# Both projections by w_phi in plain float32, one head per half of the array's rows

## The chip, the cores and the metric

The kernel runs on one core of a Trainium2 chip. The metric is device time in microseconds (us) of one execution; where several runs are given, the median counts. The engines are TensorE (PE, with its weight loads PEld), VectorE (DVE), ScalarE (ACT), GpSimd (POOL) and SyncE (SP), which issues the DMAs.

## The reference

Linear attention with a feature map, followed by a gated feed-forward layer, all in float32:

```python
def phi(x):                                  # x: batch 8, heads 8, sequence 576, head_dim 64
    proj = einsum('bhsd,df->bhsf', x, w_phi) # 128 features
    proj = proj - max(abs(proj), axis=-1)
    return concatenate([exp(proj), exp(-proj)], axis=-1)
q_p, k_p = phi(q), phi(k)
kv = einsum('bhsf,bhsd->bhfd', k_p, v)
z = sum(k_p, axis=2)
x = einsum('bhsf,bhfd->bhsd', q_p, kv) / (einsum('bhsf,bhf->bhs', q_p, z) + 1e-6)
# x reshaped to 4608 tokens x 512
out = (sigmoid(x @ w_gate) * (x @ w_val)) @ w_out   # 1536 hidden features
```

## The kernel before

The 64 heads are worked on in 32 pairs (`b, p`). A pair's Q and K lie with their features in the partitions: head 0 in partitions 0 to 63, head 1 in 64 to 127, the sequence along the free axis (576 for Q; for K four blocks of 128 and a fifth that holds both heads' last 64 positions side by side). `w_phi` is laid out as `wk`, 128 x 384, three blocks of 128 columns: [w; 0], [0; w] and [w; w] (upper half; lower half). The first two keep the heads apart in a product over all 128 partitions, since the zeros drop the other head.

Precision comes in two forms. A plain float32 product shows as two records on PE. A split product takes operands rounded to `F32R` and the remainders, `split(h, l, x)`: ACT copies x into h, rounding it, and DVE subtracts to get l; the product is then a sum of several `F32R` products of one record each.

`att_k(b, p)` (K side). For the first eight pairs (`WHOLE`), each of K's four blocks is one plain product with `wk[:, :256]` (L316), which gives both heads' 128 features for 128 positions. For the other 24 pairs K is split into `kh`, `kl` and each block is three `F32R` products with the split `wq`. Two blocks fill one PSUM bank, so group g = 0 holds blocks 0 and 1 of both heads, g = 1 blocks 2 and 3, and g = 2 the fifth block (L321, plain in all pairs). For each group DVE takes the maximum `mx` (L325) and, after the first four pairs, subtracts it (`dk`, L344); ACT takes the exponentials `ek` (L338 or L350). Ten plain products with V accumulate `kvp` (L358), which is copied, transposed (`tp`, L367) and copied again.

`att_q(b, p)` (Q side). Four pieces: two halves `hf` of the sequence (288 each) times two heads. For the first eight pairs a piece is one plain product with the [w; 0] or [0; w] block (L397). For the others, `s` ("stack", named `sq`) is built for each head: its rounded values in its own 64 partitions (ACT, L387), and the remainders in the other 64 (DVE, L388); two `F32R` products over all 128 partitions, with the two parts of `wq`'s [w; w] block, make the piece (L403). ACT copies each piece to `d` (L407); DVE finds the maxima over features and subtracts them (L413 to L428).

`att_num` multiplies the exponentials of Q by the KV state (`nm`, L456), `att_norm` and `att_scale` divide by the denominator, by way of DRAM for a broadcast, and write x to DRAM (`xs`).

The pool of PSUM banks for both projections, `ps_p`, has three buffers (tag "pp"); a pair takes seven from it, three for K and four for Q.

The feed-forward has 12 blocks of 128 hidden features. The first five (`JA`) run beside the attention as units of `mm_in` (L136, tile `gv`) and `mm_out` (L143, tile `acc`), started when a batch's x is complete; the other seven run after it, over 512 tokens at a time (tiles `g`, `v`, `acc`). The order of instructions on each engine is made by the framework's scheduler from program order and priorities: attention steps are issued under `high_priority` and the feed-forward units, handed out by `fill()`, take the room between. `issue_after(marks...)` holds some scheduling (the weights' unpacking, `att_scale`) behind DVE's subtraction in `att_q`.

Of the kernel before, what the change touches and what calls it, by code (L numbers as in the profile page):

```python
# [8 lines left out]
F32 = mybir.dt.float32  # L9
F32R = mybir.dt.float32r  # L10
# [3 lines left out]
ALU = mybir.AluOpType  # L14
AX = mybir.AxisListType
PSUM = bass.MemoryType.PSUM
DRAM = bass.MemoryType.DRAM

B, H, S, D = 8, 8, 576, 64
F = 128  # L20
P = 128
NP = H // 2
# [8 lines left out]
HS = S // 2  # L31
KVW = D + 1

JA = 5  # feed-forward blocks that run beside the attention
JR = 8  # blocks JA to JR - 1 take the attention's bytes, the others phase 1's
WHOLE = 8  # first pairs: plain float32 products, no splits
DIRECT = 4  # first pairs: K's exponentials straight from PSUM
PRIORITY = 400
RATE, LAG = 0.7, 2  # feed-forward units per slot; slots from x to its first unit


@with_exitstack
def attention_moe(
# [9 lines left out]
    nc = tc.nc  # L53
    vec, act, pool = nc.vector, nc.scalar, nc.gpsimd
# [4 lines left out]
    def split(h, l, x):  # L59
        a = act.copy(h, x)  # L60
        return a, vec.tensor_tensor(l, x, h.bitcast(F32), op=ALU.subtract)  # L61
# [2 lines left out]
        for m in marks:  # L64
            stack.enter_context(tc.issue_after(m.ins))

# [1 line left out]
    weights = {}  # L68

    ebias = const.tile([P, 1], F32, name="ebias")  # L70
    vec.memset(ebias, -896.0 * 2.0**23)

    def from_f64(h, l, raw, mid, sp, nb, name):
        # h: the value cut to 12 bits; l: the other bits as an integer times their unit
        words = raw.rearrange("p (n two) -> p n two", two=2)
        lo, hi = words[:, :, 0], words[:, :, 1]
        top = sp.tile([P, DM], U32, tag="wtop", name="wtop" + name, bufs=nb)
        vec.tensor_scalar(top, hi, 0x7FFFFE00, None, op0=ALU.bitwise_and)
        relu = act.activation(top, top, AF.Relu, bias=ebias, scale=8.0)
        vec.scalar_tensor_tensor(  # L80
            top, hi, 0x80000000, top, op0=ALU.bitwise_and, op1=ALU.bitwise_or
        )
        vec.tensor_copy(h, top.bitcast(F32))
        if mid is None:
            rest, unit = hi, lo
            vec.tensor_scalar(
                hi, hi, 16, 0x01FF0000, op0=ALU.logical_shift_left, op1=ALU.bitwise_and
            )
            vec.scalar_tensor_tensor(
                hi, lo, 16, hi, op0=ALU.logical_shift_right, op1=ALU.bitwise_or  # L90
            )
        else:
            words = mid.rearrange("p (n two) -> p n two", two=2)
            rest, unit = words[:, :, 0], words[:, :, 1]
            vec.tensor_scalar(rest, rest, 0x01FFFFFF, None, op0=ALU.bitwise_and)
        vec.tensor_scalar(unit, top, 0xFF800000, None, op0=ALU.bitwise_and)
        return relu, vec.scalar_tensor_tensor(
            l, rest, 2.0**-36, unit.bitcast(F32), op0=ALU.mult, op1=ALU.mult
        )

    def load_weights(j, m, wp, sp, nb, twice):
        if m == 0:
            wh = wp.tile([P, 3 * DM], F32R, tag=f"wh{j}", name=f"wh{j}")
            wl = wp.tile([P, 3 * DM], F32R, tag=f"wl{j}", name=f"wl{j}")
            weights[j] = (wh, wl)
        wh, wl = weights[j]
        ms = slice(m * DM, m * DM + DM)
        raw = sp.tile([P, 2 * DM], U32, tag="wraw", name=f"wraw{j}_{m}", bufs=nb + 1)
        load, mid = nc.sync.dma_start(raw, w_moe[j, :, m, :].bitcast(U32)), None
        if twice:  # L110
            # the same rows two bytes on: a word then holds the bits below h's
            mid = sp.tile([P, 2 * DM], U32, tag="wmid", name=f"wmid{j}_{m}", bufs=nb)
            nc.sync.dma_start(
                mid[:, : 2 * DM - 1].bitcast(U16),
                w_moe[j, :, m, :].bitcast(U16)[:, 1 : 4 * DM - 1],
            )
        return load, *from_f64(wh[:, ms], wl[:, ms], raw, mid, sp, nb, f"{j}_{m}")
# [135 lines left out]
            xs = nxt  # L253
        out_step(*late)

# [1 line left out]
    with ExitStack() as actx:  # L257
        wp1 = actx.enter_context(tc.tile_pool(name="wp1", bufs=1))
        moe = actx.enter_context(tc.tile_pool(name="moe1", bufs=2))
        at1 = actx.enter_context(tc.tile_pool(name="at1", bufs=1, side="right"))  # L260
        at = actx.enter_context(tc.tile_pool(name="at", bufs=2, side="right"))
        ps_gv = actx.enter_context(tc.tile_pool(name="ps_gv", bufs=2, space=PSUM))
        ps_p = actx.enter_context(tc.tile_pool(name="ps_p", bufs=3, space=PSUM))
# [5 lines left out]
        make_identity(nc, ident)  # L269
        wk = at1.tile([P, 3 * F], F32, name="wk")  # L270
        nc.sync.dma_start(wk, w_phi)
        wq = at1.tile([P, 2, 3 * F], F32R, name="wq")
        split(wq[:, 0, :], wq[:, 1, :], wk)
        dens = [
            dram.tile([2, S], F32, tag=f"den{i}", name=f"den{i}") for i in range(B * NP)
        ]
# [16 lines left out]
        def att_k(b, p):  # L293
            n = f"{b}_{p}"
            kx, vx = loaded.pop(("kv", b, p))
            kvp = ps_kv.tile([KVW, 2, 2 * F], F32, tag="kvp", name="kvp" + n)
            es = []
            whole = b * NP + p < WHOLE
            if not whole:
                kh = at.tile([P, 4 * P], F32R, tag="kh", name="kh" + n, bufs=2)  # L300
                kl = at.tile([P, 4 * P], F32R, tag="kl", name="kl" + n, bufs=2)
                split(kh, kl, kx[:, : 4 * P])
            for g in range(3):
                pp = ps_p.tile([P, 4, F], F32, tag="pp", name=f"pk{n}_{g}")
                if g < 2:
                    ns = 4
                    for i in range(2):
                        o = pp[:, 2 * i : 2 * i + 2, :].rearrange("p a f -> p (a f)")
                        ts = slice((2 * g + i) * P, (2 * g + i + 1) * P)
                        terms = [(kx, wk[:, : 2 * F])] if whole else [  # L310
                            (kh, wq[:, 0, : 2 * F]),
                            (kh, wq[:, 1, : 2 * F]),
                            (kl, wq[:, 0, : 2 * F]),
                        ]
                        for t, (x, w) in enumerate(terms):
                            nc.tensor.matmul(  # L316
                                o, x[:, ts], w, start=t == 0, stop=t == len(terms) - 1
                            )
                else:
                    ns = 1  # L320
                    nc.tensor.matmul(  # L321
                        pp[:, 0, :], kx[:, 4 * P :], wk[:, 2 * F :], start=True, stop=True
                    )
# [7 lines left out]
                    bufs=2 if ns > 1 else 2,  # L331
# [10 lines left out]
                else:  # L342
# [4 lines left out]
                        op=ALU.subtract,  # L347
# [7 lines left out]
            for hd in range(2):  # L355
                for t in range(5):
                    slot = 2 * t + hd
                    nc.tensor.matmul(  # L358
                        kvp[:, hd, :], vx[:, slot, :],
                        es[t // 2][:, slot % 4 if t < 4 else 0, :],  # L360
                        start=t == 0, stop=t == 4,
                    )
            kvt = at.tile([KVW, 4, F], F32, tag="kvt", name="kvt" + n, bufs=1)
# [14 lines left out]
        def att_q(b, p):  # L378
            n = f"{b}_{p}"
            x = loaded.pop(("q", b, p))  # L380
            early = b * NP + p < WHOLE
            if not early:
                s = at.tile([P, 2, S], F32R, tag="stack", name="sq" + n)
                for hd in range(2):
                    own = slice(hd * D, hd * D + D)
                    oth = slice(D - hd * D, P - hd * D)
                    act.copy(s[own, hd, :], x[own])  # L387
                    vec.tensor_tensor(  # L388
                        s[oth, hd, :], x[own], s[own, hd, :].bitcast(F32), op=ALU.subtract
                    )  # L390
            d = at.tile([P, 2, S], F32, tag="d", name="d" + n)
            for hf in range(2):
                for hd in range(2):
                    cs = slice(hf * HS, hf * HS + HS)
                    pp = ps_p.tile([P, HS], F32, tag="pp", name=f"pq{n}_{hf}{hd}")
                    if early:
                        nc.tensor.matmul(  # L397
                            pp, wk[:, hd * F : hd * F + F], x[:, cs],
                            start=True, stop=True,
                        )  # L400
                    else:
                        for i in range(2):
                            nc.tensor.matmul(  # L403
                                pp, wq[:, i, 2 * F :], s[:, hd, cs],
                                start=i == 0, stop=i == 1,
                            )
                    act.copy(d[:, hd, cs], pp)  # L407
            nj = 2 * S // 32
            pm = at.tile([P, nj], F32, tag="pm", name="pm" + n)
            pn = at.tile([P, nj], F32, tag="pn", name="pn" + n)  # L410
# [4 lines left out]
                op=ALU.max, apply_absolute_value=True, apply_transpose=True,  # L415
# [4 lines left out]
            for a in range(4):  # L420
                o = a ^ 1
# [216 lines left out]
```

## Time and profile before

| | |
|---|---|
| median of 3 runs | 1304.68 us (1303.23 to 1305.15) |
| profiled execution, its span | 1307.2 us |
| mean granted TensorE clock | 0.992 |
| PE / PEld busy | 1269.8 / 1070.8 us |
| DVE / ACT busy | 877.5 / 650.7 us |
| DMA moved | 125.12 MB |
| first eight pairs' projections (L397, the last start) | to 124.6 us |
| last projection record (L321, start) | 648.2 us |

The profile is of one execution. Busy time is the union of an engine's records; on PE records overlap, so a record's mean duration is longer than the spacing of a stream of such records. A row of instruction groups reads: line, engine, operation, tiles out<-in, shapes, count | busy us, mean ns of one | idle time of the engine just before them and what ended it. In the shapes of a product, 128*65 stands for a stationary operand of 128 rows and 65 columns. "f32" stands for `F32R` operands too.

### The profile page before, as it was taken

Reading aid. Unit: us, or ns where it says so; the run is one execution under the profiler, and the core shown is the slowest. Engines: PE = TensorE matmul, PEld = TensorE weight load, DVE = VectorE, ACT = ScalarE, POOL = GpSimd, SP = SyncE. Lnnn points to the kernel's source line nnn. Section 1 sums busy time; section 2 is a strip of 40 time slices with the busy share of each in tenths; the row PEclk is TensorE's granted clock in tenths of the full one; section 3 lists DMA queues with packets and bytes.
Section 4 is the critical chain, followed back from the end, with each engine's and each line's share of the span. In section 5 each row is a group of like instructions: output and inputs, shape, how many; then the busy total and the mean of one; then the engine's idle time right before and its main releaser. Section 6 shows DMA issues by size and latency. Waiting matters only on the chain.

```text
span 1307.2 us, 19107 instructions
## 1 busy us (share of the span) xinstructions
PE 1269.8 (97%) x7112; PEld 1070.8 (82%) x7112; DVE 877.5 (67%) x1778; ACT 650.7 (50%) x1416; POOL 0.6 (0%) x6
## 2 busy tenths in 40 slices
PE   7878999999999999999999999999999999999998
PEld 4545788999898989898998988888888888888886
DVE  5777989899899888989866958834343443434333
ACT  5754777777777787777754523322222222222221
POOL 0000000000000000000000000000000000000000
PEclk9988999999999999999999999999999999999999
DMA  5576543233233323332225424313021211202010
GB/s 190 165 216 195 167 131 100 85 107 105 86 115 86 107 84 118 94 108 76 61 69 180 130 78 132 97 65 97 1 97 33 65 50 48 97 1 97 1 65 33
DMA packets 75166, 125.12 MB, mean 96 GB/s; under 512 B 18496, under 2 KB 38080, under 8 KB 75072
## 3 DMA queue, kind: packets, MB, share of 16 engines
q1 hardware_dynamic: 75072, 123.89, 30.7%
q8 instruction: 56, 0.92, 0.3%
q14 instruction: 38, 0.31, 0.1%
HBM read 95.25 MB, written 28.46 MB: 95 GB/s over the span
## 4 chain that ended last, share of the span: by engine, by line
PE 88%; DVE 4%; DMA 4%; ACT 2%; issue 1%; SPq 0%; DVEq 0%; ACTq 0%
PE acc L143 22%; PE gv L136 17%; PE g L136 13%; PE v L136 13%; PE kvp L358 9%; PE nm L456 7%; PE pk L316 3%; PE pq L403 2%; PE pq L397 1%; DMA xs<-xp 1%; DMA q<-q 1%; DMA rb<-den 1%; DMA dn<-ex 1%; ACT ek L338 1%; DMA wraw<-w_moe 1%
## 5 line engine op out<-in xcount | busy, mean ns | idle before, releaser
L136 PE MATMUL gv<-xh,wh 128*128 128x256 f32 x720 | 208.3, 290 | 3.6 <-DVE t L156 3.4
L136 PE MATMUL gv<-xh,wl 128*128 128x256 f32 x720 | 206.5, 287 | 0.0
L136 PE MATMUL gv<-xl,wh 128*128 128x256 f32 x720 | 206.2, 286 | 0.0
L60 ACT CAST hh<-u 128x256 fp32r<-128x256 f32 (+1 forms) x153 | 75.4, 494 | 245.3 <-DVE u L157 245.1
L143 PE MATMUL acc<-wh,hh 128*128 128x512 f32 x432 | 171.3, 397 | 0.7 <-ACT y L187 0.7
L143 PE MATMUL acc<-wl,hh 128*128 128x512 f32 x432 | 169.9, 393 | 0.0
L143 PE MATMUL acc<-wh,hl 128*128 128x512 f32 x432 | 166.1, 394 | 0.1
L358 PE MATMUL kvp<-ek,v 128*65 128x256 f32 x640 | 158.6, 383 | 6.9 <-ACT ek L338 5.3
L155 DVE TENSOR_SCALAR t<-t 128x256 uint32<-128x256 uint32 (+1 forms) x153 | 52.5, 344 | 154.6 <-ACT t L152 153.7
L136 PEld LDWEIGHTS gv<-xh,wh 128*128 128x128 f32 x720 | 137.1, 191 | 10.0 <-DVE t L156 4.7
L136 PEld LDWEIGHTS gv<-xl,wh 128*128 128x128 f32 x720 | 137.0, 190 | 3.3
L136 PEld LDWEIGHTS gv<-xh,wl 128*128 128x128 f32 x720 | 137.0, 190 | 2.3
L358 PEld LDWEIGHTS kvp<-ek,v 128*65 128x65 f32 x640 | 86.6, 138 | 49.4 <-ACT ek L338 9.7
L61 DVE TENSOR_TENSOR hl<-u,hh 128x256 fp32r<-128x256 f32 (+1 forms) x153 | 81.1, 531 | 47.2 <-ACT hh L60 46.1
L152 ACT ACTIVATE t<-g 128x512 f32<-128x512 f32 x63 | 37.6, 597 | 150.0 <-PE g L136 149.8
L156 DVE SCALAR_TENSOR_TENSOR t<-t,v 128x512 f32<-128x512 f32 x63 | 43.3, 687 | 85.6 <-PE v L136 85.4
L136 PE MATMUL g<-xh,wh 128*128 128x512 f32 x252 | 99.0, 393 | 0.0
L136 PE MATMUL v<-xh,wh 128*128 128x512 f32 x252 | 98.6, 391 | 0.0
L136 PE MATMUL g<-xl,wh 128*128 128x512 f32 x252 | 98.6, 391 | 0.0
L136 PE MATMUL g<-xh,wl 128*128 128x512 f32 x252 | 98.5, 391 | 0.0
L136 PE MATMUL v<-xl,wh 128*128 128x512 f32 x252 | 98.3, 390 | 0.0
L136 PE MATMUL v<-xh,wl 128*128 128x512 f32 x252 | 98.2, 390 | 0.0
(91 smaller groups left out, 2533.6 us busy)
## 6 DMA issues: line engine op xcount, KB each, us to landing
wraw<-w_moe SPq DMA_DIRECT2D x36, 512.0 KB, 3.9
xl<-xs SPq DMA_DIRECT2D x36, 512.0 KB, 4.1
v<-v SPq DMA_DIRECT2D x32, 325.0 KB, 3.3
k<-k SPq DMA_DIRECT2D x32, 320.0 KB, 3.1
q<-q SPq DMA_DIRECT2D x32, 288.0 KB, 3.2
rb<-den SPq DMA_DIRECT2D x32, 288.0 KB, 3.8
ys<-y SPq DMA_DIRECT2D x36, 256.0 KB, 2.1
yp<-ys SPq DMA_DIRECT2D x36, 256.0 KB, 4.3
```

Of the source, the lines that this page charges most:

```text
L60: a = act.copy(h, x)
L61: return a, vec.tensor_tensor(l, x, h.bitcast(F32), op=ALU.subtract)
L136: nc.tensor.matmul(o, a[:, ws], x[:, cs], start=i == 0, stop=i == 11)
L143: nc.tensor.matmul(acc, a[:, ts], w[:, ws], start=first and i == 0, stop=last and i == 2)
L152: act.activation(t, g, AF.Tanh, scale=0.5)
L155: vec.tensor_scalar(tu, tu, 0x7FFFFFFF, None, op0=ALU.bitwise_and)
L156: vec.scalar_tensor_tensor(t, t, 1.0, vl, op0=ALU.add, op1=ALU.mult)
L316: nc.tensor.matmul(o, x[:, ts], w, start=t == 0, stop=t == len(terms) - 1)
L338: act.activation(e[:, i, sg * F : sg * F + F], pp[:, i, :], AF.Exp, bias=(mn, mx)[sg][:, i : i + 1], scale=1.0 - 2.0 * sg,)
L358: nc.tensor.matmul(kvp[:, hd, :], vx[:, slot, :], es[t // 2][:, slot % 4 if t < 4 else 0, :], start=t == 0, stop=t == 4,)
L403: nc.tensor.matmul(pp, wq[:, i, 2 * F :], s[:, hd, cs], start=i == 0, stop=i == 1,)
L456: nc.tensor.matmul(nm, a[:, 2 * hd + sg, :], x[:, hd, :], start=sg == 0 and i == 0, stop=sg == 1 and i == last,)
```

## The change

In `att_k`, for all 32 pairs, K's first four blocks are projected by plain float32 products over 64 partitions each: head 0 from partitions 0 to 63, head 1 from 64 to 127, both with their half of the [w; w] block. The two heads' products alternate block by block and write two different PSUM banks, one for each head; a group g = 0 or 1 is now a head with its four blocks, where it was two blocks of both heads. In `att_q`, for all pairs, each half of the sequence is two plain products over 64 partitions, one for each head, into two banks, issued one after the other and then copied. The splits of K, Q and `w_phi` (`kh`, `kl`, `s`, `wq`) go. The fifth block of K, V's products, `att_num` and the feed-forward stay as they are. The diff also drops some comments.

```diff
-        wq = at1.tile([P, 2, 3 * F], F32R, name="wq")
-        split(wq[:, 0, :], wq[:, 1, :], wk)
...
-            whole = b * NP + p < WHOLE
-            if not whole:
-                kh = at.tile([P, 4 * P], F32R, tag="kh", name="kh" + n, bufs=2)
-                kl = at.tile([P, 4 * P], F32R, tag="kl", name="kl" + n, bufs=2)
-                split(kh, kl, kx[:, : 4 * P])
+            pps = [
+                ps_p.tile([P, 4, F], F32, tag="pp", name=f"pk{n}_{hd}") for hd in range(2)
+            ]
+
+            for t in range(4):
+                for hd in range(2):
+                    own = slice(hd * D, hd * D + D)
+                    nc.tensor.matmul(
+                        pps[hd][:, t, :], kx[own, t * P : t * P + P], wk[own, 2 * F :],
+                        start=True, stop=True,
+                    )
             for g in range(3):
-                pp = ps_p.tile([P, 4, F], F32, tag="pp", name=f"pk{n}_{g}")
                 if g < 2:
-                    ns = 4
-                    for i in range(2):
-                        o = pp[:, 2 * i : 2 * i + 2, :].rearrange("p a f -> p (a f)")
-                        ts = slice((2 * g + i) * P, (2 * g + i + 1) * P)
-                        terms = [(kx, wk[:, : 2 * F])] if whole else [
-                            (kh, wq[:, 0, : 2 * F]),
-                            (kh, wq[:, 1, : 2 * F]),
-                            (kl, wq[:, 0, : 2 * F]),
-                        ]
-                        for t, (x, w) in enumerate(terms):
-                            nc.tensor.matmul(
-                                o, x[:, ts], w, start=t == 0, stop=t == len(terms) - 1
-                            )
+                    ns, pp = 4, pps[g]
                 else:
                     ns = 1
+                    pp = ps_p.tile([P, 4, F], F32, tag="pp", name=f"pk{n}_{g}")
...
-                        es[t // 2][:, slot % 4 if t < 4 else 0, :],
+                        es[hd][:, t, :] if t < 4 else es[2][:, 0, :],
...
-            early = b * NP + p < WHOLE
-            if not early:
-                s = at.tile([P, 2, S], F32R, tag="stack", name="sq" + n)
+            d = at.tile([P, 2, S], F32, tag="d", name="d" + n)
+            for hf in range(2):
+                cs = slice(hf * HS, hf * HS + HS)
+                pps = [
+                    ps_p.tile([P, HS], F32, tag="pp", name=f"pq{n}_{hf}{hd}")
+                    for hd in range(2)
+                ]
                 for hd in range(2):
                     own = slice(hd * D, hd * D + D)
-                    oth = slice(D - hd * D, P - hd * D)
-                    act.copy(s[own, hd, :], x[own])
-                    vec.tensor_tensor(
-                        s[oth, hd, :], x[own], s[own, hd, :].bitcast(F32), op=ALU.subtract
-                    )
-            d = at.tile([P, 2, S], F32, tag="d", name="d" + n)
-            for hf in range(2):
+                    nc.tensor.matmul(
+                        pps[hd], wk[own, 2 * F :], x[own, cs], start=True, stop=True
+                    )
                 for hd in range(2):
-                    cs = slice(hf * HS, hf * HS + HS)
-                    pp = ps_p.tile([P, HS], F32, tag="pp", name=f"pq{n}_{hf}{hd}")
-                    if early:
-                        nc.tensor.matmul(
-                            pp, wk[:, hd * F : hd * F + F], x[:, cs],
-                            start=True, stop=True,
-                        )
-                    else:
-                        for i in range(2):
-                            nc.tensor.matmul(
-                                pp, wq[:, i, 2 * F :], s[:, hd, cs],
-                                start=i == 0, stop=i == 1,
-                            )
-                    act.copy(d[:, hd, cs], pp)
+                    act.copy(d[:, hd, cs], pps[hd])
```

## The prediction

> **What bounds the kernel now.** I read the page first (shares and chain), then the busy time by stage, then the list of what TensorE waited for in the saturated stage, then single pitches in the chain.
>
> ```profile
> span 1307.2 us, 19107 instructions
> PE 1269.8 (97%) x7112; PEld 1070.8 (82%) x7112; DVE 877.5 (67%) x1778; ACT 650.7 (50%) x1416; POOL 0.6 (0%) x6
> PE 88%; DVE 4%; DMA 4%; ACT 2%; issue 1%; SPq 0%; DVEq 0%; ACTq 0%
> ```
>
> TensorE (PE) carries 88% of the chain that ended last. By stage:
>
> ```profile
> 100.00:120.00 20.00, 15.42 (x68) 10.20 (x67) 15.49 (x33) 9.90 (x20) 0.00 (x0) 0.83 0.71 233
> 120.00:140.00 20.00, 18.88 (x112) 14.69 (x112) 17.65 (x42) 11.02 (x27) 0.00 (x0) 1.00 0.62 179
> 140.00:160.00 20.00, 19.60 (x127) 16.08 (x126) 19.75 (x40) 13.12 (x31) 0.00 (x0) 1.00 0.57 165
> 300.00:400.00 100.00, 100.00 (x690) 89.88 (x689) 90.18 (x189) 74.16 (x168) 0.00 (x0) 1.00 0.32 95
> 500.00:600.00 100.00, 100.00 (x683) 89.49 (x682) 87.86 (x181) 75.41 (x170) 0.00 (x0) 1.00 0.35 102
> ```
>
> The columns are PE, its weight loads (PEld), DVE, ACT, POOL, the granted clock, DMA. Up to about 118 us the first eight pairs run with gaps on every engine; from 160 us PE has no gap. The waits of PE from 160 to 760 us are these two rows and nothing else:
>
> ```profile
> PE gv L136 <- DVE t L156: 3.4, 4, 1.4
> PE pq L403 <- DVE sq L388: 0.3, 1, 0.3
> ```
>
> So for pairs 8 to 31 the currency is PE time: feed-forward products fill whatever attention leaves, and a microsecond added to PE moves the end by a microsecond. A microsecond taken off DVE or ACT there buys at most those 3.7 us in all, although DVE is 90% busy.
>
> **Pitch, not duration.** Records of PE overlap, so a record's mean duration is not its price. The chain shows stretches of one kind, start, length, count:
>
> ```profile
> 67.00 1.73 PE pk L316 x8
> 83.63 0.48 PE pq L397 x2
> 192.24 0.27 PE pq L403 x2
> 192.86 0.54 PE pq L403 x4
> 195.49 0.32 PE pq L403 x2
> 195.92 1.44 PE pk L316 x12
> 619.39 0.53 PE pq L403 x4
> 626.23 0.22 PE pk L321 x2
> ```
>
> Rounded products (one record each): K's 128x256 take 1.44/12 = 0.120 us, Q's 128x288 take 0.53/4 = 0.133 us. Plain float32 products leave two records each (four early products of K per pair, and x64 for eight pairs below): a record of 256 columns takes 1.73/8 = 0.216 us, of 288 columns 0.48/2 = 0.24 us, of 128 columns 0.22/2 = 0.11 us. The rows at 192 to 196 us are one pair's projections: four stretches with other work between them.
>
> **The change, part by part.**
>
> ```profile
> L316 PE MATMUL pk<-wk,k 128*128 128x256 f32 x64 | 15.3, 379 | 0.0
> L316 PE MATMUL pk<-wq,kh 128*128 128x256 f32 x192 | 36.9, 284 | 0.0
> L403 PEld LDWEIGHTS pq<-sq,wq 128*128 128x128 f32 x192 | 30.2, 189 | 2.7 <-PE pq L403 0.5
> L358 PEld LDWEIGHTS kvp<-ek,v 128*65 128x65 f32 x640 | 86.6, 138 | 49.4 <-ACT ek L338 9.7 <-ACT ek L350 2.2 <-issue 1.2
> L61 DVE TENSOR_TENSOR kl<-k,kh 128x512 fp32r<-128x512 f32 x24 | 16.4, 682 | 0.1
> L388 DVE TENSOR_TENSOR sq<-q,sq 64x576 fp32r<-64x576 f32 x48 | 36.1, 753 | 1.5
> L387 ACT CAST sq<-q 64x576 fp32r<-64x576 f32 x48 | 32.1, 668 | 0.6
> L60 ACT CAST kh<-k 128x512 fp32r<-128x512 f32 x24 | 14.8, 616 | 6.4 <-DMA k<-k 6.2
> ```
>
> 1. Late pairs (24), PE before: K 1.44 us; Q 8 x 0.133 = 1.06 us; together 2.50 us.
>
> 2. Late pairs after, without any overlap of the two halves: K has eight products of 128 columns, 16 records x 0.11 = 1.76 us; Q has four of 288 columns, 8 x 0.24 = 1.92 us. Sum 3.68 us, or +1.18 us a pair and +28.3 us in all. A product over 64 rows streams as many columns as one over 128, so the half-height alone saves nothing; only running head 0 beside head 1 does.
>
> 3. How much overlaps. No row here has products on two halves, so this is bounded. Program order is head 0 first record, second record, head 1 first, second. The best order-keeping overlap runs head 1's first beside head 0's second: K in 9 steps instead of 16 (0.99 us), Q in 3 steps per half of the sequence instead of 4 (6 x 0.24 = 1.44 us, or 5 steps, 1.20 us, where the halves touch). The other end is item 2. Between them I go by the weight loads:
>
> ```profile
> 621.50 0.28 PE L136 MATMUL gv<-xh,wh 128*128 128x256 f32 x1
> 621.50 0.14 PEld L456 LDWEIGHTS nm<-eql,kvh 128*65 128x65 f32 x1
> 621.62 0.29 PE L456 MATMUL nm<-eql,kvh 128*65 128x288 f32 x1
> 621.62 0.19 PEld L136 LDWEIGHTS gv<-xl,wh 128*128 128x128 f32 x1
> 621.99 0.29 PE L136 MATMUL gv<-xh,wh 128*128 128x256 f32 x1
> 622.01 0.37 PEld L367 LDWEIGHTS tp<-ident,kvt 65*128 65x128 f32 x4
> 622.11 0.41 PE L367 MATMUL tp<-ident,kvt 65*128 65x65 f32 x4
> 622.33 0.36 PE L136 MATMUL gv<-xl,wh 128*128 128x256 f32 x1
> ```
>
> A load starts when the product before it starts, one ahead. From 189 and 138 ns for 128 and 65 columns, a column costs 51/63 = 0.81 ns, so 128 columns hold the load path for an estimated 0.10 us. (The transposes' loads of 65 rows come four in 0.37 us, so a cheaper load of half the rows isn't excluded.) With loads one ahead and one at a time, K's 0.11 us records are paced by their loads: nothing gained, 1.76 us. In Q, head 1's first record starts 0.10 us after head 0's second, not 0.24 us: 0.24 + 0.10 + 0.24 + 0.24 = 0.82 us a half, 1.65 us a pair. I take this: 1.76 + 1.65 = 3.41 us, +0.91 us on 2.50 us, x24 = **+21.9 us**. I take it because the one-ahead loads are in the trace, and more than that is not.
>
> 4. Changing the array between whole and halved. Four stretches a pair make eight changes, 192 over the late pairs. The nearest row is the change to the transposes and back (65 rows) at 621.99 to 622.33 us: the first comes 0.12 us after its predecessor, four take 0.22 us, no gap; so 0 is the low end. The high end is the tail of a record that pitch hides: 0.28 - 0.12 = 0.16 us (621.50 and 621.62), if the next form has to wait for it, which is +31 us. I take 0.03 us, near the row that exists: **+5.8 us**.
>
> 5. Early pairs (8), PE before 1.73 + 1.92 = 3.65 us, after 3.41 us: at most -1.9 us. Against it, DVE's first maximum of K waited for four records (0.87 us), and now for 14 of 16 (1.54 us), since both heads finish together: at most 8 x 0.67 = +5.4 us. PE and DVE both have gaps there, so I take 0 between -2 and +5.
>
> 6. Rounding removed: DVE loses 0.68 + 2 x 0.75 = 2.19 us a pair, ACT 0.62 + 2 x 0.67 = 1.95 us. From 160 us on the cover is PE, so nothing; between 118 and 160 us DVE is the chain and four of these pieces lie on it:
>
> ```profile
> 137.72 0.60 DVE kl L61
> 141.56 0.76 DVE sq L388
> 143.74 0.75 DVE sq L388
> 168.06 0.75 DVE sq L388
> ```
>
> Together **-2.9 us**; after them DVE's own queue (the weights' unpacking and K's maxima) is next. All three pairs there at full price would be 6.6 us; none, if DMA takes over, 0. The split of w_phi is a single pair of instructions beside the first loads: 0. No DMA is added, removed or moved on any queue.
>
> 7. Banks: K now asks two of the pool's three banks at once, as Q does. Seven allocations a pair stay seven. With DVE and ACT relieved I cost this at 0; if that cover fails, PE waits for a reader, up to the 0.67 us of a maximum per pair.
>
> Sum: 21.9 + 5.8 - 2.9 = +24.8 us on the profiled 1307.2 us, 1332.0 us. The median of the runs, 1304.68 us, is 2.5 us under the span, so **1329.5 us**. Its own range runs from full overlap of products with loads in line (K 1.76, Q 1.20: +0.46 x 24 = 11.0, with items 4 and 6 +13.9, 1318.6 us) to no overlap (28.3 + 5.8 - 2.9 = +31.2, 1335.9 us, and 1340 with item 5's delay).
>
> **Rivals.**
>
> A, the other side: the halves truly run side by side, loads included. Late pairs 0.99 + 1.44 = 2.43 us (-1.7 us in all), or 0.99 + 1.20 = 2.19 us (-7.4 us); early pairs 3.65 to about 2.4 us, -10 us, of which half may reach the end, -5; rounding -2.9. Sum -10 to -15 us, 1290 to 1295 us, if changing the array is free. Against it: the loads above. For it: separate rows and banks, and the transposes' quick loads. It decides at 0.05 to 0.08 us per change of the array (10 to 15 us over 192); above that even this case isn't faster. The Trainium skill, page "TensorE: Matmul & The Clock Gate", Part 3, has four row tiles at 3.07 times the speed with starts about 4 ns apart; by that rule this rival holds, and no run here shows it yet.
>
> B: each change of the array waits for the tail, 0.16 us. 21.9 + 30.9 - 2.9 = +49.9 us, 1354.6 us; with no overlap 1361 us. Against it: the transposes pass without a gap. For it: they use more than half of the rows, so they may be no change at all. The Trainium skill, page "TensorEngine Tiling (Array Packing)", section Tiling Modes, Key Properties, says that changing the mode, not just the tile, drains the engine; by that this rival holds, and no row of before can show it.
>
> C: the change does not do what it says and the halves run strictly in turn: item 2, 1335.9 us, inside the forecast's own range.
>
> **Chances.** The forecast with C 0.50, A 0.20, B 0.25, the rest (bank waits, a schedule that PE cannot follow) 0.05. Slower by over 0.2% (2.6 us, what a measurement of this kernel can tell): forecast, B, the rest, and a fraction of A with costly changes, 0.77. Within: the part of A near its break-even, 0.07. Faster: the rest of A, 0.16. The range leaves out a tenth at each end: 1296 (into A) to 1358 us (into B).
>
> **What would show it.** After: each projection record of K at 0.11 us pitch and Q's head 1 starting 0.10 us after head 0's second (item 3); starts nearly equal would be A. A gap of 0.1 to 0.2 us between a projection and its neighbours, both ways, would be B. PE's waits from 160 us stay a few us; the sq and kl rows vanish and DVE's 90% falls near 80% with no gain from it. I am wrong if the loads of the two halves overlap, if changes cost far from 0.03 us, or if the first eight pairs move by more than 5 us.

## The result, and the profile after

The changed kernel takes 1359.53 us (median of 4 runs, 1358.02 to 1361.91) against 1304.91 us (4 runs): the ratio is 1.0418, 95% interval 1.0401 to 1.0434. It is 54.6 us slower. The forecast was 1329.5 us, 24.8 us slower, with a range from 1296 to 1358 us. One run among those below, of the kernel with plain products over the whole array, was granted a clock of 0.848, took 1446.47 us and is left out of that kernel's time.

The page of the changed kernel, total and chain:

```profile
span 1356.8 us, 19238 instructions
PE 1327.8 (98%) x7272; PEld 1060.2 (78%) x7272; DVE 832.7 (61%) x1705; ACT 621.3 (46%) x1343; POOL 0.6 (0%) x6
PE 89%; DMA 5%; DVE 4%; ACT 1%; issue 1%; SPq 0%; DVEq 0%
```

The busy time by stage (PE, PEld, DVE, ACT, POOL, granted clock, DMA share, GB/s), for the two saturated stretches that were shown of before:

```profile
300.00:400.00 100.00, 100.00 (x629) 78.77 (x630) 73.25 (x156) 64.29 (x145) 0.00 (x0) 1.00 0.31 90
500.00:600.00 100.00, 100.00 (x628) 78.48 (x627) 71.72 (x152) 63.64 (x142) 0.00 (x0) 1.00 0.29 88
```

The clock is granted in full, PE shows no idle time and DVE has fallen from 90% to 73%. But the loads fell from 90% to 79%, and in 100 us PE gets through 629 records where it did 690. What PE waited for from 160 to 760 us is as little as before:

```profile
PE gv L136 <- DVE t L156: 1.8, 2, 1.6
PE acc L143 <- ACT y L187: 0.7, 1, 0.7
PE pq L382 <- PE nm L435: 0.4, 1, 0.4
PE pq L382 <- DVE dk L336: 0.2, 1, 0.2
```

So PE hardly waits for another engine, and the time lies between its own records. The timeline of the changed kernel around one lone Q product (start, length, engine, line, count), first the products, then the loads:

```profile
389.67 0.39 PE L143 MATMUL acc<-wl,hh 128*128 128x512 f32 x1
389.89 0.39 PE L143 MATMUL acc<-wh,hl 128*128 128x512 f32 x1
390.21 0.75 PE L382 MATMUL pq<-q,wk 64*128 64x288 f32 x2
390.89 0.50 PE L143 MATMUL acc<-wh,hh 128*128 128x512 f32 x1
391.23 0.39 PE L143 MATMUL acc<-wl,hh 128*128 128x512 f32 x1
```

```profile
390.21 0.29 PEld L382 LDWEIGHTS pq<-q,wk 64*128 64x128 f32 x2 [0.35 <-issue]
390.89 0.19 PEld L143 LDWEIGHTS acc<-wh,hh 128*128 128x128 f32 x1 [0.39 <-issue]
391.00 0.19 PEld L143 LDWEIGHTS acc<-wl,hh 128*128 128x128 f32 x1
391.23 0.19 PEld L143 LDWEIGHTS acc<-wh,hl 128*128 128x128 f32 x1
```

An `acc` product is normally followed 0.23 us later by the next, so the stream was done at 389.89 + 0.23 = 390.12. The half products begin at 390.21, and their load begins with them, not one product ahead. After them the same happens again: load and product of `acc` both at 390.89, the next only 0.34 us later. Counted back by one pitch from 391.23, the stream is on its way again at 391.00. The stretch took 0.88 us for two records of 0.24 us: about 0.40 us went on one change into the halved array and one back.

The other side is there too. Where half products of different halves stand side by side, they run side by side:

```profile
400.44 0.51 PE L382 MATMUL pq<-q,wk 64*128 64x288 f32 x1
400.45 0.60 PE L303 MATMUL pk<-wk,k 64*128 64x128 f32 x3
400.79 0.40 PE L382 MATMUL pq<-q,wk 64*128 64x288 f32 x1
400.88 0.49 PE L303 MATMUL pk<-wk,k 64*128 64x128 f32 x3
401.31 0.46 PE L359 MATMUL tp<-ident,kvt 65*128 65x65 f32 x4
401.70 0.93 PE L303 MATMUL pk<-wk,k 64*128 64x128 f32 x8
```

```profile
400.44 0.18 PEld L382 LDWEIGHTS pq<-q,wk 64*128 64x128 f32 x1
400.45 0.18 PEld L303 LDWEIGHTS pk<-wk,k 64*128 64x128 f32 x1
```

A Q product and a K product start 0.01 us apart, and so do their loads. The view doesn't name the halves; that these two lie in different ones follows from the kernels below, where products of the same half do not start together.

The transposes at 401.31 us, over 65 rows, stand between half products here. From the first of them to the next half product it is 0.39 us; among whole products four of them took 0.22 us (622.11 to 622.33 us in the profile before). So products over 65 rows count as whole ones: going between them and halves costs time, going between them and products over 128 rows did not.

In the program's order on PE, half products form 162 stretches with whole products between them. 75 of these are a single Q product with no partner: one head's product is issued when its own bank is free, and the other's comes later, with other whole products in between. That the separate banks are the reason is borne out by the kernel with both banks in one tile, below: it has 10 such stretches.

### The profile page after: what moved, and what is told of

It is laid out like the page before. It is cut to its first block, busy times and chain, and to the rows that moved or that the text cites. A ratio compares the mean times of both kernels' runs of the same rounds, so it can differ in the third digit from the quotient of the medians.

```text
span 1356.8 us, 19238 instructions
## 1 busy us (share of the span) xinstructions
PE 1327.8 (98%) x7272; PEld 1060.2 (78%) x7272; DVE 832.7 (61%) x1705; ACT 621.3 (46%) x1343; POOL 0.6 (0%) x6
## 4 chain that ended last, share of the span: by engine, by line
PE 89%; DMA 5%; DVE 4%; ACT 1%; issue 1%; SPq 0%; DVEq 0%
PE acc L143 21%; PE gv L136 17%; PE g L136 13%; PE v L136 13%; PE kvp L350 9%; PE nm L435 6%; PE pq L382 5%; PE pk L303 3%; DMA rb<-den 2%; DMA dn<-ex 1%; DMA den<-dn 1%; DVE xp L463 1%; DMA wmid<-w_moe 1%; PE tp L359 1%; PE pk L313 1%
## 5 line engine op out<-in xcount | busy, mean ns | idle before, releaser
L382 PE MATMUL pq<-q,wk 64*128 64x288 f32 x256 | 90.7, 476 | 6.6 <-DMA q<-q 4.1
```

Of the source, the lines that this page charges most:

```text
L382: nc.tensor.matmul(pps[hd], wk[own, 2 * F :], x[own, cs], start=True, stop=True)
```

## Experiments

Theory D: the loss is the changes of the array (from whole to halved and back), about 0.39 us a stretch of half products, while products in two halves overlap as hoped. Rival S: the loss is the plain products' own time, in turn, with free changes. Differences below are to the median of the kernel before on the same chip (1304.9 to 1305.4 us).

### The price of a change, by itself: four kernels

All four are the kernel before with 126 extra products in the second phase, where no attention runs.

```diff
# whole / lone: r = 0:P  /  0:D ahead of g, D:P ahead of vl
+                nc.tensor.matmul(g, weights[j][0][r, :P], xs[0][r, :CW], start=True, stop=True)
                 mm_in(g, xs, j, 0, CW)
+                nc.tensor.matmul(vl, weights[j][0][r, :P], xs[0][r, :CW], start=True, stop=True)
                 mm_in(vl, xs, j, 1, CW)
# pair / same: both extra products ahead of mm_in(g, ...), rows 0:D and D:P  /  0:D twice
```

Whole: 

> Control: the kernel before, with 126 extra F32R products of 128 rows x 512 columns in the second phase (one ahead of each of the 126 gate and value sums, into the same bank, overwritten by the sum's first product). Both theories: 126 x 0.2315 = +29.2 us, 1334 us.

Lone: 

> As the control, but each extra product uses 64 rows only, alone between products over 128 rows: 252 changes of the array, no plain float32 and no attention in it. Theory D: 126 x (0.2315 + 0.39) = +78.3 us, 1383 us. Rival S (a change of the array is free): as the control, 1334 us.

Pair: 

> As the lone products, but the two of a unit stand together, rows 0 to 63 into one bank and rows 64 to 127 into another: 63 stretches, 126 changes. Theory D with overlap: 63 x (0.39 + 0.24) = +39.7 us, 1344.6 us. Theory D without overlap: 63 x (0.39 + 0.463) = +53.7 us, 1358.6 us. Rival S: 1334 us, or 1319.5 us if the halves overlap.

Same half: 

> As the pair of half products in the second phase, but both use rows 0 to 63: 63 stretches, 126 changes, nothing that could run side by side. Theory D: 63 x (0.39 + 2 x 0.2315) = +53.7 us, 1359 us, 13 to 14 us over the run with two different halves (1345.8 us), and that difference is the overlap. If halves do not overlap: as that run, 1346 us, with a change of the array then costing 0.28 us a stretch, which the lone products (+80 us) contradict.

Measured 1334.38, 1385.54, 1345.79 and 1359.50 us. The differences to before are +29.0, +80.2, +40.4 and +54.6 us, so:

- a whole product costs 29.0/126 = 0.230 us; a lone half product (80.2 - 29.0)/126 = 0.406 us more, 0.203 us a change;
- of the 63 pairs the scheduler parted two, in both pair kernels, so each has 65 stretches. In two halves a stretch costs 40.4/65 = 0.622 us, no more than a lone product's 80.2/126 = 0.637 us: the second product is free;
- in the same half the 61 pairs cost (54.6 - 40.4)/61 = 0.233 us more each: the time of one more product.

A stretch pays the same changes with one product or two, 0.2 us each on average of the way in and the way out, and products of different halves overlap entirely. The rows of the lone product, and of the pair, in their kernels' timelines:

```profile
1004.77 0.39 PE L143 MATMUL acc<-wh,hl 128*128 128x512 f32 x1
1005.09 0.50 PE L243 MATMUL g<-xh,wh 64*128 64x512 f32 x1
1005.52 0.50 PE L136 MATMUL g<-xh,wh 128*128 128x512 f32 x1
1005.86 0.39 PE L136 MATMUL g<-xl,wh 128*128 128x512 f32 x1
```

```profile
1006.80 0.39 PE L143 MATMUL acc<-wh,hl 128*128 128x512 f32 x1
1007.12 0.50 PE L243 MATMUL g<-xh,wh 64*128 64x512 f32 x1
1007.12 0.50 PE L244 MATMUL v<-xh,wh 64*128 64x512 f32 x1
1007.55 0.50 PE L136 MATMUL g<-xh,wh 128*128 128x512 f32 x1
1007.89 0.40 PE L136 MATMUL g<-xl,wh 128*128 128x512 f32 x1
```

The steps from start to start are 0.32, 0.43 and 0.34 us in the first, where the stream's own step is 0.23: 0.09 + 0.20 + 0.11 = 0.40 us. In the second they are the same, with two products in the place of one. The runs give the sum; how it splits between the change there and the change back is a reading of these rows.

### Plain products over the whole array

```diff
-            whole = b * NP + p < WHOLE
+            whole = True
...
-            early = b * NP + p < WHOLE
+            early = True
```

> All 32 pairs use the plain float32 products of the early pairs, over all 128 rows with the zero blocks of wk; no half of the array is used, no splits of K and Q. Theory D (the loss of the change is the switching of the array between whole and halved, about 0.39 us a stretch of half products, not the plain products as such): K 1.73 + Q 1.92 = 3.65 us a late pair against 2.50, +27.6 us over 24 pairs, less 2.9 us of rounding: 1329.6 us, 30 us faster than the changed kernel, with plain products all the same. Rival S (the plain products' own PE time is the loss, and the halves add nothing and overlap nothing): within 5 us of the changed kernel's 1359.5 us.

Measured 1331.82 us, +26.5 us, ratio 1.0191 (1.0159 to 1.0222). Plain products for all pairs cost what the pitches say (27.6 - 2.9 = 24.7). Half of the change's loss goes when only the halving is taken away; S falls.

### K alone, Q alone

The function `att_k`, or `att_q`, of the changed kernel in the kernel before.

> Only att_k is changed; att_q stays with its F32R products. Program order has 56 stretches of K half products, 12 of all eight. Theory D with overlap inside a stretch (eight products in 0.84 us, four in 0.61 us, read from the changed kernel's trace): about 1.1 us a late pair against 1.44, -7 us, and some of the early pairs' 1.73: 1294 to 1304 us, not slower than before. Rival S: 1.76 against 1.44 us a pair, +7.7 us, 1311 us.

> Only att_q is changed; att_k stays with its F32R products. Program order has 120 stretches of Q half products, 115 of them one product alone. Theory D: four lone products at 0.87 us are 3.48 us a late pair against 1.06, +58 us over 24 pairs, less some 2 us of rounding, with early pairs adding up to 6: 1358 to 1370 us, the whole loss of the change or a little more. Rival S: 1.92 against 1.06, +20.6 us, 1324 us.

K alone: 1315.27 us, +10.0 us, ratio 1.0077 (1.0047 to 1.0107). That misses what D said (no slower), by a misreading: the 0.84 us it priced eight products with was read from stretches of eight records, which are four products. Over its clear stretches after 160 us K takes 36.5 us for 22.7 pairs' worth of records, 1.61 us a pair against 1.44, or +4 us; the other 6 us lie outside these stretches. Q alone: 1365.73 us, +60.4 us, ratio 1.0453 (1.0425 to 1.0481), as D said and 42 us over S: 115 of its 120 stretches are one lone product. Q carries the loss. The two don't add up to the change's 54.6 us; in the changed kernel 24 stretches hold K and Q products together, and each of the two kernels has a changed order in the first pairs, which the next runs look at.

### The first eight pairs

> The change in the first eight pairs alone; pairs 8 to 31 as before. Theory D: PE has gaps there, a pair's K costs less and its Q more: 1300 to 1312 us. Rival E (the loss of the change comes from the early pairs' longer chain, since both heads' K end together): +20 us or more, over 1325 us.

Measured 1318.78 us, +13.5 us, ratio 1.0088 (1.0055 to 1.0121): more than D said, less than the rival. Then the same order of K without any change of the array:

```diff
+                    nc.tensor.matmul(     # first eight pairs, for t in range(4), for hd in range(2)
+                        pps[hd][:, t, :], kx[:, t * P : t * P + P],
+                        wk[:, hd * F : hd * F + F], start=True, stop=True,
+                    )
```

> The kernel before, but the first eight pairs group K's projection by head, with eight plain products of 128 columns over the whole array (blocks [w;0] and [0;w]) instead of four of 256: the same PE time (16 records of 0.11 us), no change of the array, but both groups of K ready late, as in the change. Theory L (the loss of the change in the first eight pairs alone, 13.5 us, is the later first maximum of K): 1310 to 1319 us. Theory D (it is the changes of the array there): 1303 to 1307 us. Theory O (it comes from the different program order and its single waits, whatever the cause): somewhere else, between 1300 and 1320 us, with waits of other pieces in the trace.

Measured 1312.80 us, +7.9 us, ratio 1.0052 (1.0034 to 1.0069). So by the medians over half of this loss comes without a change of the array, from grouping K by head (theories L and O together; the run does not part them). The two intervals are wide enough for this to be all of it, or less than a third. And the loss is not taken in the first pairs themselves: in the kernel with early halves the products with V of the ninth pair start at 160.6 us, and before at 160.5 us; the first feed-forward product starts 4.4 us later (120.6 against 116.2 us), but the 600th product into `gv` is level with before (326.6 against 326.8 us). The 800th, at 405.7 against 397.0 us, is 8.7 us behind. Most of the loss thus comes between these two, where PE has a single long wait, for `xh`, that the kernel before does not have (waits of PE, 160 to 760 us):

```profile
PE gv L136 <- DVE t L156: 4.4, 2, 2.7
PE gv L136 <- ACT xh L60: 3.8, 1, 3.8
```

The wait for `xh`, which itself waits 2.7 us for the DMA into `xl`, is at 370 to 380 us, and behind it the granted clock was 0.51 from 375 to 380 us and 0.80 from 380 to 385 us. This is one execution, 2.3 us slower than the median. What the changed order does there was not followed further.

### Both heads held together

The two heads' banks become one tile of two banks, so neither head starts alone:

```diff
-            pps = [
-                ps_p.tile([P, 4, F], F32, tag="pp", name=f"pk{n}_{hd}") for hd in range(2)
-            ]
+            two = ps_p.tile([P, 2, CW], F32, tag="two", name=f"pk{n}")
+            pps = [two[:, hd, :].rearrange("p (a f) -> p a f", f=F) for hd in range(2)]
```

and the same in `att_q`; the pool has one buffer of it and one bank for K's fifth block.

> The changed kernel, with the two heads' banks taken as one tile of two banks (one buffer, and one bank for K's fifth block), so that neither head's products can start before both banks are free. Program order then has 109 stretches against 162, 58 of them the two heads' Q products together. Theory D: a pair of Q products together costs 0.83 us instead of 2 x 0.87; some 34 such merges after the early pairs save 31 us: 1320 to 1335 us. Rival W (waits for banks are the loss): fewer buffers make it slower than 1360 us. Rival S: no change, 1355 to 1360 us.

> Pairs 8 to 31 take both projections by halves, with the two heads' banks as one tile of two banks; the first eight pairs stay as before, with their three single banks (the pool is exchanged between them). Program order has 81 stretches, 45 of them the two heads' Q products together and 18 all of K. Theory D: 81 x 0.39 = 31.6 us of changes, products at 0.90 us for K and 0.98 us for Q a pair, 45 us, together 77 us against 24 x 2.50 = 60; less 2.9 us of rounding: 1319 us (1313 to 1325). Rival S (plain products in turn, changes free): +28.3 - 2.9, 1331 us. If the first eight pairs carried the rest of the two-bank kernel's loss, 1352 - 1319 = 33 us is theirs.

All pairs: 1352.01 us, ratio 1.0352 (1.0333 to 1.0370), 7.5 us faster than the change but 17 us over what D said. Its first feed-forward product starts 26 us later than in the kernel before: one buffer seems to starve the first pairs, whose work is a chain (up to 160 us PE waits 17.5 us for ACT's `ex`, where it waited 2.8 us before). The rows of tile `gv` (count, least/median/longest ns, first and last start), of before and of this kernel:

```profile
L136 PE MATMUL gv<-xh,wh x720: 274/283/579, 116.2 to 774.0; 128*128 128x256 f32 x180
```

```profile
L136 PE MATMUL gv<-xh,wh x720: 274/283/497, 142.3 to 817.4; 128*128 128x256 f32 x180
```

With the first eight pairs as before: 1332.47 us, +27.6 us, ratio 1.0204 (1.0182 to 1.0226), 27 us faster than the change with the same products in the later pairs; some of that may belong to the first pairs, which the change takes by halves. In its timeline both heads' Q together and all of K's eight products read:

```profile
404.74 0.40 PE L143 MATMUL acc<-wh,hl 128*128 128x512 f32 x1
405.07 0.76 PE L535 MATMUL pq<-q,wk 64*128 64x288 f32 x4
405.75 0.50 PE L143 MATMUL acc<-wh,hh 128*128 128x512 f32 x1
...
409.59 0.28 PE L136 MATMUL gv<-xh,wl 128*128 128x256 f32 x1
409.80 1.16 PE L402 MATMUL pk<-wk,k 64*128 64x128 f32 x16
410.89 0.39 PE L136 MATMUL gv<-xh,wh 128*128 128x256 f32 x1
411.11 0.28 PE L136 MATMUL gv<-xl,wh 128*128 128x256 f32 x1
```

Four Q records span 0.76 us where two spanned 0.75 us: the second head is free once the array is halved. K's 16 records take from 409.71 to 410.99, 1.28 us with both changes, against 1.76 us in turn and 1.44 us of the split products. D's sum for this kernel was 13 us too low. Over its later stretches a pair's projections take 3.30 us (75.0 us of stretches for 22.7 pairs' worth of records), +0.80 us on 2.50 us, or +19 us; the other 8 us are not settled, apart from somewhat longer waits for `t` (6.5 us from 160 to 900 us).

Last, K alone that way, for the later pairs:

> Only K of pairs 8 to 31 by halves, with the two banks as one tile; Q's F32R products use the same tile; the first eight pairs as before. Program order has 32 stretches, 16 of all eight products. Theory D: 32 x 0.39 + 24 x 0.90 = 34.1 us against 24 x 1.44 = 34.6, less about 1 us of rounding: 1303.5 us, same as before to within 5 us of order effects. Rival S: +7.7 us, 1313 us.

Measured 1415.88 us, ratio 1.0843 (1.0827 to 1.0859): a miss by 112 us that tells nothing of the changes. The longest waits of PE:

```profile
PE kvp L449 <- ACT ek L441: 23.1, 17, 3.4
PE gv L136 <- ACT xh L60: 17.9, 2, 16.7
PE nm L551 <- ACT ex L555: 16.9, 21, 2.3
```

PE waits for ACT here, with Q's split products sharing the one two-bank buffer. That the buffer is the reason is not shown, and why it does no such harm when both projections are by halves was not tried. No version came out faster than the kernel before.

## Why the prediction was wrong

**The bound: right.** From 160 us on PE time is the currency; relieving DVE by 17 points and ACT by 10 (in part because a pair takes longer) bought nothing that shows.

**Item 4, the changes: the step that failed.** It took eight changes a pair at 0.03 us, +5.8 us. Over the 116 stretches after 160 us that stand clear of one another (102.6 us by the reckoning shown for the lone Q product, holding 21.9 pairs' worth of records), a pair has 5.3 stretches, 10.6 changes. At 0.203 us each, the price from the kernels above, that is 2.15 us a pair, 51.6 us over 24 pairs. (The change's own lone Q products agree: 0.88 us for 0.48 us of records, 0.40 us for two changes.) Both factors were too small. The price went by the transposes, on 65 rows; those count as whole, as the rows at 401.31 us show, so that row was evidence of nothing. Its upper end, 0.16 us, held only the tail of the last product. By the rows, 0.09 us goes before the load and product start, and 0.11 us more for the load that is not made ahead. The count went by the stretches of before, where a product alone cost nothing. The changed kernel has 162 stretches over 32 pairs.

**Item 3, the overlap: too pessimistic.** It took 3.41 us a pair, with loads one at a time. The 102.6 us leave 4.68 - 2.15 = 2.53 us for the products, near rival A's 2.43 and hardly above the 2.50 of before. Loads of the two halves do run beside each other, and products start together where they are neighbours.

**Item 5, early pairs: it left out what follows them.** It took 0 with an upper end of +5. For the pairs themselves that holds: in the changed kernel the first feed-forward product starts 3.7 us later than before (119.9 against 116.2 us), and the ninth pair's products with V 0.9 us earlier (159.6 against 160.5 us). But a change of order alone, in the first pairs, made the whole kernel 7.9 us slower, and halves there 13.5 us, the latter mostly after 330 us. How much of such a loss the changed kernel has is open; beside the sum for the late pairs, below, there is little room for it.

**Item 6:** the rounding's -2.9 us can't be told apart in any run. **Item 7:** the banks cost as waits nothing (the list of waits), but they part the two heads' products, and so make the stretches.

Late pairs by this: (4.68 - 2.50) x 24 = +52.3 us of the 54.6. So the result is rival B's mechanism, at a higher price and more often, on top of rival A's overlap. B's 1354.6 to 1361 us holds the measured time, but by two errors that cancel: it had less overlap and fewer changes. Rival A's break-even of 0.05 to 0.08 us a change was the right question, and 0.2 us answers it.

The Trainium skill, page "TensorEngine Tiling (Array Packing)", section Tiling Modes, Key Properties, says that a change of mode drains the engine; the trace agrees in that each change costs time, 0.203 us. I gave the rival that goes by it a chance of 0.25 for want of a row; a rule that speaks against a change, when the only row for the change does not bear on it, deserved more. The Trainium skill, page "TensorE: Matmul & The Clock Gate", Part 3, has the tiles' products start some 4 ns apart; the pair at 1007.12 us agrees (3 to 4 ns in all 61 pairs of that trace).

Two slips in the working do not bear on this: 192 x 0.16 us is 30.7 us, where rival B's sum has 30.9; and the forecast, B and the rest already make 0.80, so a chance of 0.77 for "slower" left no room for them and a part of A.

## What to carry to other kernels

In this kernel's terms, price half-array products by the stretch, not by the product: a stretch costs 0.41 us before it does anything, and inside it a second half is free. It pays only where the products that it saves are longer than that and nothing stands between them. Count stretches in the order that will be issued; a scheduler that starts each head when its own bank is free parts what was meant to run together, and one tile over both banks keeps them together. A nearest row is a bound only if it does the thing: ask first whether the transpose on 65 rows changes the array at all.

## What was not expected of the hardware

A change of the array costs about 0.2 us, on average of both directions, though PE's busy share stays at 100%: the loss hides in records that look longer (0.50 us for 0.39), and in the loads, whose busy share falls (90% to 79%). Halves overlap entirely, loads included (with the two changes, 0.622 us for a stretch of two products and 0.637 us for a stretch of one), and plain float32 records of two halves overlap as `F32R` products do (0.76 us for four Q records, 0.75 us for two).
